# Activation table loaded first, one diagonal score group computed in full, last weights loaded at other points of the schedule

## The chip, the cores and the metric

The kernel runs on one core of a Trainium2 chip. The metric is the device time of one execution in microseconds (us). The engines are called by their profile names: PE is TensorE, DVE is VectorE, ACT is ScalarE, POOL is GpSimd (it issues most of the loads from memory here), SP is SyncE (it issues the transposing transfers here). An instruction issued to a queue for a transfer carries a q, as in SPq.

Kernels are compared by a ratio: the mean time of one kernel's fast runs over the mean of the other's fast runs of the same rounds. So a gain quoted from a ratio is not quite the difference of the medians. Gains in us are (1 - ratio) x 1260.

## The reference, cut to what matters

```python
# attention part: 8 batches, S = 3008 rows, D = 256, z has 64 columns
scores = (1.0 / S) * np.matmul(z, z.transpose(0, 2, 1))   # symmetric
attn = np.maximum(scores, 0.0) ** 2
x = (u * np.matmul(attn, v)).reshape(B * S, D)
# feed-forward part, d_ff = 2048
h = x @ moe_w_in
g = h * np.cos(h)
out = g @ moe_w_out
```

## The kernel before

Each batch is cut into 6 columns of 512 rows (c) and 6 row blocks of 512 (R); the last of each has 448. A group (b, c, R) is a 512x512 piece of the symmetric attention matrix: four matmuls, Relu, square, into a tile `a`. Off the diagonal, only the groups with R > c are computed as a rule, and the mirrored piece comes from a transposing transfer (`tt<-a`, a 512x512 tile). In the first three columns of batch 0 (`direct`) all groups are computed.

A diagonal group (R == c) is symmetric in itself. The kernel computes its upper part and mirrors the rest with three small transposing transfers inside the tile (`a<-a`), except in the `direct` columns:

```python
def direct(b, c, R):
    return b == 0 and c <= 2

def s_matmuls(b, c, R, p):
    ...
    diagonal = R == c and not direct(b, c, R)
    for k in ((0, 1), (3, 2) if diagonal else (2, 3))[p]:
        s0 = k if diagonal else 0          # diagonal: 512, 384, 256, 128 columns
        ...

def s_squares(b, c, R, p, banks):
    ...                                    # a tile from a ring of 9
    diagonal = R == c and not direct(b, c, R)
    if diagonal:
        for i in range(2):
            k = 2 * p + i
            nc.scalar.activation(rt[:, i, k * P:], banks[k][:, k * P:], AF.Relu)   # L240
            nc.vector.tensor_tensor(...)                                           # L241, the squares
            if k < K - 1:
                nc.sync.dma_start_transpose(                                       # L245, a<-a
                    t[:, k + 1:, k, :],
                    t[:, k, k + 1:, :].rearrange("p s w -> p (s w)"))
        ...
        return
    for i in range(2):
        ...
            nc.scalar.activation(rt[:, i, :], banks[k], AF.Relu)                   # L256
    nc.vector.tensor_tensor(...)                                                   # L258, the squares
    if p == 1:
        ...
        if R > c and not direct(b, R, c):
            nc.sync.dma_start_transpose(tt..., t...)                               # L265, tt<-a
```

The cosine is the Sin function with a bias of pi/2 (L348), followed by a product on DVE (`g`, L351). The order of PE is fixed by the program; each step has a time t, in which a column takes 8 units. A load is released when PE has reached the step before it. PE lines to know: L223 scores, L310 attention products, L344 input matmuls (x times w_in), L361 output matmuls (g times w_out).

```python
            for q in range(4):
                at(4 + 2 * q, 0, lambda q=q: load_w_in(q))
                at(15 + 2 * q, 0, lambda q=q: load_w_out(q))
        else:
            at(t - 3.5 * U, 0, lambda b=b: load_z(b))      # U = 8
    ...
    def prepare():
        nc.scalar.activation(dummy, pihalf, AF.Relu)       # first instruction of ACT
```

## Time and profile before

| | kernel before |
|---|---|
| median of 3 runs | 1260.18 us |
| span in the profile | 1256.7 us |
| PE busy | 99% of the span |
| waits of PE, all in the first 84 us | 14.7 us |

From the page of the kernel before: the first line is busy time and share of the span; the other two cut the span into 40 slices, with the busy share and the granted clock of PE in tenths.

```profile
PE 1238.2 (99%) x7533; PEld 680.4 (54%) x7533; DVE 782.0 (62%) x1391; ACT 845.6 (67%) x1610; POOL 146.0 (12%) x201
...
PE   8879999999999999999999999999999999999998
...
PEclk9979999999999999999999999999999999999999
```

PE has no room except in the first three slices (31 us each), and the third slice has a clock of 7 tenths. The waits of PE in the kernel before (who waited, for whom, us in all, times, longest):

```profile
PE acc L310 <- DMA a<-a: 6.4, 3, 5.1
PE w L223 <- DVE g L351: 3.0, 6, 1.3
PE acc L310 <- DVE x L331: 1.3, 1, 1.3
...
PE w L344 <- DVE g L351: 0.8, 1, 0.8
```

The largest wait is for the small transposes of a diagonal group. Which one, the timelines show. First PE in order of time (start, us, engine, line, operation, count; in brackets the idle time before it and what ended it):

```profile
63.07 3.30 PE L344 MATMUL w<-x,w_in_70 128*128 128x512 f16 x8 [0.75 <-DVE g L351]
66.21 0.38 PE L310 MATMUL acc<-a,v_66 128*128 128x512 f16 x1
71.65 0.59 PE L310 MATMUL acc<-a,v_66 128*128 128x512 f16 x1 [5.06 <-DMA a<-a]
72.92 0.59 PE L310 MATMUL acc<-a,v_66 128*128 128x512 f16 x1 [0.68 <-DMA a<-a]
74.19 2.29 PE L310 MATMUL acc<-a,v_66 128*128 128x512 f16 x5 [0.68 <-DMA a<-a]
...
84.46 0.60 PE L361 MATMUL w<-w_out_71,g 128*128 128x256 f16 x4
```

The products of column 3 begin at 66.21 us and stop after one matmul. Then the queue of SP, for the same stretch:

```profile
40.92 28.22 SPq L265 DMA_TRANSPOSE tt<-a  x5
69.31 3.74 SPq L245 DMA_TRANSPOSE a<-a  x3
73.10 4.19 SPq L265 DMA_TRANSPOSE tt<-a  x2
```

The three `a<-a` transposes of column 3's diagonal group are issued from 69.31 us on, after five large `tt<-a` transposes that held the queue for 28.22 us. DVE had the squares ready long before:

```profile
53.53 1.02 DVE L241 TENSOR_TENSOR a<-rt 128x512 f16<-128x512 f16 x4
59.33 0.69 DVE L258 TENSOR_TENSOR a<-rt 128x1024 f16<-128x1024 f16 x1 [4.79 <-DMA tt<-a]
...
63.53 1.89 DVE L258 TENSOR_TENSOR a<-rt 128x1024 f16<-128x1024 f16 x3
```

The squares of the diagonal group (L241) ended at 54.55 us. Then DVE stood 4.79 us, because its next group needed an `a` tile that a `tt<-a` transfer was still reading. ACT, at the same time:

```profile
49.11 1.28 ACT L348 ACT_TABLE_LOAD   x1
50.41 0.69 ACT L348 ACTIVATE c_661<-w,pihalf 128x512 f16<-128x512 f32 x1
```

A table load of 1.28 us stands before the first cosine. The windows view gives, for each stretch, its length, then the busy us of PE, PEld, DVE, ACT and POOL (instructions in brackets), then the granted clock, DMA share and GB/s.

```profile
61.00:62.00 1.00, 0.55 (x4) 0.18 (x2) 1.00 (x3) 1.00 (x3) 0.00 (x0) 1.00 1.60 158
62.00:63.00 1.00, 0.32 (x2) 0.10 (x1) 1.00 (x3) 1.00 (x3) 0.00 (x0) 0.78 1.56 169
63.00:64.00 1.00, 0.93 (x3) 0.37 (x3) 1.00 (x3) 1.00 (x3) 0.00 (x0) 0.50 1.51 194
...
77.00:78.00 1.00, 1.00 (x4) 0.31 (x3) 0.00 (x0) 0.00 (x0) 0.00 (x0) 0.50 1.15 218
```

The clock was halved twice: from about 62.6 to 66 us and from about 69.4 to 79.6 us (the edges are worked out from the mean clock of the stretches that hold them). The first of these stretches is 3.41 us long, the second 10.23 us. In the PE timeline, eight matmuls of L344 take 3.30 us at 63.07 us, where eight at full clock take 1.89 us.

### The profile page before, as it was taken

How to read it: one execution, taken by the hardware profiler on the slowest of the kernel's cores; microseconds unless marked ns; L12 is line 12 of the kernel's file. 1: busy time of each engine (PE TensorE's matmuls, PEld its weight loads, DVE VectorE, ACT ScalarE, POOL GpSimd, SP SyncE). 2: the span in 40 equal slices, each digit the busy share in tenths (PEclk: the TensorE clock that was granted, in tenths of full speed). 3: DMA queues.
4: the chain of work that ended last, by engine and by line, in shares of the span. 5: the costliest groups of instructions: out<-in, count | busy, mean ns of one | idle time of the engine just before them, and what ended most of it. 6: DMA issues, size and time to landing. Idle time of an engine off the chain costs nothing.

```text
span 1256.7 us, 20414 instructions
## 1 busy us (share of the span) xinstructions
PE 1238.2 (99%) x7533; PEld 680.4 (54%) x7533; DVE 782.0 (62%) x1391; ACT 845.6 (67%) x1610; POOL 146.0 (12%) x201
## 2 busy tenths in 40 slices
PE   8879999999999999999999999999999999999998
PEld 3335555555555555555555555555555555555556
DVE  8646656666666666666656666666666666666555
ACT  6646766667766676667766666776767666677646
POOL 3300101101020010200101001010010101100000
PEclk9979999999999999999999999999999999999999
DMA  9977858778576795868958679676695856957311
GB/s 162 161 127 132 130 98 118 122 122 133 104 111 116 118 133 107 121 119 114 135 97 116 122 124 141 90 122 113 116 146 102 116 110 109 156 94 113 71 33 44
DMA packets 485076, 145.05 MB, mean 115 GB/s; under 512 B 433264, under 2 KB 484976, under 8 KB 484976
## 3 DMA queue, kind: packets, MB, share of 16 engines
q1 hardware_dynamic: 357312, 88.92, 42.7%
q0 software_dynamic: 100400, 29.77, 24.1%
q10 hardware_dynamic: 27264, 25.06, 6.3%
q8 instruction: 59, 0.97, 0.3%
q14 instruction: 41, 0.34, 0.1%
HBM read 60.29 MB, written 24.64 MB: 68 GB/s over the span
## 4 chain that ended last, share of the span: by engine, by line
PE 96%; DMA 2%; DVE 1%; ACT 0%; SPq 0%; issue 0%; DVEq 0%
PE acc L310 37%; PE w L361 26%; PE w L344 26%; PE w L223 6%; DMA tt<-a 1%; PE acc L285 1%; DMA ut<-ust_62 1%; DVE g L351 0%; DMA x<-in_z_dram 0%; SPq L245 0%; DMA a<-a 0%; ACT zT_63 L196 0%; DVE a L258 0%; DVE x L331 0%; ACT rt L256 0%
## 5 line engine op out<-in xcount | busy, mean ns | idle before, releaser
L344 PE MATMUL w<-x,w_in_70 128*128 128x512 f16 x1504 | 447.9, 381 | 0.8 <-DVE g L351 0.8
L361 PE MATMUL w<-w_out_71,g 128*128 128x256 f16 x3008 | 448.6, 273 | 0.0
L361 PEld LDWEIGHTS <-g 128*128 128x128 f16 x3008 | 294.2, 98 | 191.6 <-issue 1.4
L256 ACT ACTIVATE rt<-w 128x512 f16<-128x512 f32 x485 | 251.2, 614 | 119.7 <-PE w L223 119.7
L258 DVE TENSOR_TENSOR a<-rt 128x1024 f16<-128x1024 f16 x252 | 172.4, 691 | 182.5 <-ACT rt L256 177.3
L344 PEld LDWEIGHTS <-w_in_70 128*128 128x128 f16 x1504 | 147.6, 98 | 61.1 <-issue 7.3
L90 POOL DMA_DIRECT2D ust_62<-in_u_dram x64 | 44.8, 704 | 400.1 <-PE acc L310 389.1
L240 ACT ACTIVATE rt<-w 128x512 f16<-128x512 f32 (+3 forms) x180 | 64.3, 449 | 39.8 <-PE w L223 39.8
L310 PEld LDWEIGHTS <-v_66 128*128 128x128 f16 x552 | 52.1, 98 | 68.4 <-issue 21.6
L310 PE MATMUL acc<-a,v_66 128*128 128x512 f16 x312 | 81.3, 385 | 7.7 <-DMA a<-a 6.4
L331 DVE TENSOR_TENSOR x<-acc,ut 128x64 f16<-128x64 f32 (+7 forms) x178 | 69.7, 432 | 27.7 <-PE acc L310 26.6
L310 PE MATMUL acc<-a,v_65 128*128 128x512 f16 x336 | 85.8, 380 | 0.0
L310 PEld LDWEIGHTS <-v_67 128*128 128x128 f16 x552 | 52.1, 98 | 59.3 <-issue 12.3
L310 PEld LDWEIGHTS <-v_65 128*128 128x128 f16 x552 | 51.6, 98 | 59.8 <-issue 12.2
L310 PEld LDWEIGHTS <-v_68 128*128 128x128 f16 x552 | 51.9, 98 | 57.7 <-issue 10.9
L310 PE MATMUL acc<-a,v_67 128*128 128x512 f16 x312 | 80.0, 383 | 0.0
L310 PE MATMUL acc<-a,v_68 128*128 128x512 f16 x312 | 79.2, 379 | 0.0
L368 ACT ACTIVATE ob<-w 128x256 f32<-128x256 f32 x188 | 73.0, 388 | 5.3 <-PE w L361 5.3
L241 DVE TENSOR_TENSOR a<-rt 128x512 f16<-128x512 f16 (+3 forms) x180 | 48.4, 322 | 44.1 <-ACT rt L240 44.1
L90 POOL DMA_DIRECT2D ust_61<-in_u_dram x48 | 36.5, 765 | 227.3 <-PE acc L310 219.8
L310 PE MATMUL acc<-tt,v_68 128*128 128x512 f16 (+1 forms) x240 | 62.2, 371 | 0.0
L310 PE MATMUL acc<-tt,v_67 128*128 128x512 f16 (+1 forms) x240 | 62.1, 371 | 0.0
(1547 smaller groups left out, 1400.1 us busy)
## 6 DMA issues: line engine op xcount, KB each, us to landing
out_dram<-ob ACTq DMA_DIRECT2D x92, 256.0 KB, 2.3
ust_61<-in_u_dram POOLq DMA_DIRECT2D x48, 128.0 KB, 4.0
ust_62<-in_u_dram POOLq DMA_DIRECT2D x32, 128.0 KB, 4.4
a<-a SPq DMA_TRANSPOSE x135, 2.9
v_65<-in_v_dram POOLq DMA_DIRECT2D x4, 512.0 KB, 6.0
v_66<-in_v_dram POOLq DMA_DIRECT2D x4, 512.0 KB, 6.5
v_68<-in_v_dram POOLq DMA_DIRECT2D x4, 512.0 KB, 6.4
v_67<-in_v_dram POOLq DMA_DIRECT2D x4, 512.0 KB, 6.1
```

Of the source, the lines that this page charges most:

```text
L90: hold(nc.gpsimd.dma_start(dst, src))
L223: chain(nc.tensor.matmul(sp[:, s0 * P:], zt[h, R * K + k + 1 - lo, :], zt[h, j0 + s0:j0 + K, :].rearrange("p j w -> p (j w)"), start=True, ...
L240: nc.scalar.activation(rt[:, i, k * P:], banks[k][:, k * P:], AF.Relu)
L241: nc.vector.tensor_tensor(t[:, k, k:, :].rearrange("p s w -> p (s w)"), rt[:, i, k * P:], rt[:, i, k * P:], ALU.mult)
L256: nc.scalar.activation(rt[:, i, :], banks[k], AF.Relu)
L258: nc.vector.tensor_tensor(t.rearrange("p s k w -> p k s w")[:, 2 * p:2 * p + 2], rv, rv, ALU.mult)
L285: chain(nc.tensor.matmul(accs[(b, c)][nh], vs(b, NG - 1)[h, G - 1, nh * P:(nh + 1) * P], a[h], start=False, stop=False))
L310: chain(nc.tensor.matmul(acc[nh][:, 0:wn], vs(b, j // G)[:, j % G, nh * P:(nh + 1) * P], a, start=(n == 0), stop=(n == NJ - 2)))
L331: nc.vector.tensor_tensor(x[:, nh, :], acc[nh][:, o:o + n], ut[:, nh, o:o + n], ALU.mult)
L344: chain(nc.tensor.matmul(hp, w_in16[:, k, ft * P:(ft + 1) * P], x[:, k, :], start=(k == 0), stop=(k == NDH - 1)))
L361: chain(nc.tensor.matmul(ys[m][:, 0:D], gs[(m, f4)][:, ft % FG, ts * P:(ts + 1) * P], w_out16[:, ft, :], start=(ft == 0), stop=(ft == NFT ...
L368: nc.scalar.activation(obs[m][:, i, :], ys[m][:, 0:D], AF.Copy, bias=0.0, scale=inv_s2)
```

## The change

Its intent: (A) load the table that holds the cosine at the start, where ACT has nothing to do; (B) compute column 3's diagonal group of batch 0 in full, so that it needs no transpose; (C) load the last weights, w_out, later, out of the way of the transposes. The whole diff:

```diff
@@ s_matmuls and s_squares
-        diagonal = R == c and not direct(b, c, R)
+        diagonal = R == c and (b, c) > (0, NC // 2)
@@ the schedule
-                at(15 + 2 * q, 0, lambda q=q: load_w_out(q))
+                at(17 + 2.5 * q, 0, lambda q=q: load_w_out(q))
@@ prepare
-        nc.scalar.activation(dummy, pihalf, AF.Relu)
+        nc.scalar.activation(dummy, pihalf, AF.Sin)
```

NC // 2 is 3, so the first line changes group (0, 3, 3) alone.

## The prediction

> **What bounds the kernel now.** TensorE: the page gives PE 99% of a 1256.7 us span, and the chain that ended last is 96% PE. After 84 us the view of waits shows no wait of PE at all. All that can be won lies before. There its waits sum to 14.7 us: 6.4 us for the transposes of a diagonal group ("DMA a<-a"), 3.8 us for VectorE's g, the rest mostly start-up.
>
> To this comes the clock. The windows view shows a granted clock of 0.50 from 62.3 to 66 us and from 70 to 79.5 us; 512-wide matmuls then stand 0.42 us apart instead of 0.22. The Trainium skill, "TensorE: Matmul & The Clock Gate" (Part 1), says the array halves its clock after about 3.4 us of idleness and needs as long a busy stretch to get it back; this trace agrees (half soon after the gap from 66.6 to 71.6 us, full 5 us after steady work resumes at 74.2). Estimate of what it costs: 3.6/2 + 5.3/2 = 4.4 us.
>
> **The parts of the change.**
>
> 1. Diagonal group of column 3 in full. Its three transposes wait in the SyncE queue behind five large tt transposes (40.9 to 69.1 us, 4 to 7.6 us each): squares ready at 54.5 us, transposes issued at 69.3 to 71.9 us. Without them PE goes on at 66 us. Removed: 6.4 us of wait and the second cold stretch, 2.6 us. Added: 768 matmul columns (under 0.3 us), and about a microsecond of ScalarE and VectorE.
>
> 2. The cosine table first. ScalarE's timeline shows two table loads of 1.28 us, at 1.27 us (nobody waits) and at 49.1 us, before the first cosine; none later, though Relu, Copy and Sin mix, so one should do. The Trainium skill, "ScalarE: Activation LUTs" (What ACT_TABLE_LOAD costs), gives 1283 ns; the trace agrees. PE waits 0.51 + 0.38 + 0.33 us behind it. Gain: 1.2 us.
>
> 3. w_out later. Four 256 KB loads are issued at 41.7 to 52.0 us, 10.7 us to landing, while the transposes crawl. VectorE stands 4.8 us (54.5 to 59.3) until a tt transpose frees its a buffer; this costs PE 2.5 us and the first half-clock stretch, 1.8 us. About two loads move behind that transpose; I expect it 2 to 3 us sooner. But part 2 brings PE there 1.2 us sooner, so I count half: 2 us of 4.3. The last load will be issued near 62 us and wanted near 73 us: just enough at 10.7 us, perhaps a wait of up to 2 us.
>
> **Sum.** 6.4 + 2.6 + 1.2 + 2 - 0.3 (columns) - 0.3 (late weights) = 11.6 us, all critical, since PE runs without a gap afterwards. Predicted 1260.2 - 11.6 = 1248.6 us; range 1245.5 to 1253.0. Chances: faster by over 2%: 0.01; within 2%: 0.985; slower: 0.005.
>
> **What would show it.** Right: no "DMA a<-a" among PE's waits; one table load, at the start; PEclk's slice of 7 back at 9; first output matmul near 73 us instead of 84.5; PE's work after it unchanged. Step 3 is wrong if VectorE still stands 4 us or more for tt and half clock near 60 us remains.
>
> **What would make it wrong.** PE, arriving sooner, waits for another transfer (w_out, u or tt not landed); the Relus need a second table load; contention so tight that tt lands no sooner and swallows part 2 (then the gain is about 8 us).

## The result and the profile after

| | before | after |
|---|---|---|
| median (6 runs each) | 1260.01 us | 1246.45 us |
| lowest to highest | 1257.53 to 1262.06 | 1244.05 to 1247.43 |
| ratio of the fast runs | | 0.9892, 95% interval 0.9878 to 0.9905 |
| span in the profile | 1256.7 us | 1244.6 us |

The gain is 13.6 us, 1.08%. The page of the changed kernel, the same lines:

```profile
PE 1234.4 (99%) x7533; PEld 680.0 (55%) x7533; DVE 782.0 (63%) x1389; ACT 844.7 (68%) x1609; POOL 145.8 (12%) x201
...
PEclk9999999999999999999999999999999999999999
```

PE's work has become 3.8 us shorter although matmul columns were added: both half-clock stretches are gone in this profile. That is one execution. The record also gives the mean granted clock of every timed run, from which the time at half clock can be estimated as 2 x (1 - clock) x span. The six runs of the changed kernel have 1.000 (twice), 0.999, 0.998 and 0.997 (twice), so four of them had about 2.5 to 7.5 us of half clock somewhere. The 34 runs of the kernel before in the rounds told of below have 0.993 to 0.997, that is about 17.6 to 7.5 us; the 12 at 0.993 took 1260.7 us on average, the 8 at 0.996 or 0.997 took 1258.0. So there is much less half clock than before, but not always none.

PE's waits in the changed kernel:

```profile
PE acc L310 <- DVE x L331: 2.6, 1, 2.6
...
PE w L344 <- DVE g L351: 0.8, 1, 0.8
PE w L223 <- DVE g L351: 0.4, 2, 0.2
```

There is no `DMA a<-a` any more, and the wait of the scores for g went from 3.0 to 0.4 us. The timelines of PE, SP, DVE and ACT of the changed kernel, in this order:

```profile
62.62 1.89 PE L344 MATMUL w<-x,w_in_70 128*128 128x512 f16 x8 [0.75 <-DVE g L351]
64.34 1.89 PE L310 MATMUL acc<-a,v_66 128*128 128x512 f16 x8
66.07 1.03 PE L310 MATMUL acc<-a,v_67 128*128 128x512 f16 x4
...
72.65 0.60 PE L361 MATMUL w<-w_out_71,g 128*128 128x256 f16 x4
```

```profile
43.29 35.32 SPq L265 DMA_TRANSPOSE tt<-a  x7
```

```profile
56.13 0.69 DVE L258 TENSOR_TENSOR a<-rt 128x1024 f16<-128x1024 f16 x1 [0.28 <-ACT rt L256]
58.88 0.69 DVE L258 TENSOR_TENSOR a<-rt 128x1024 f16<-128x1024 f16 x1 [2.06 <-ACT c_739 L348]
```

```profile
1.27 1.28 ACT L465 ACT_TABLE_LOAD   x1 [1.27 <-PEq L497]
```

The products of column 3 now run through, at full clock, and the first output matmul stands at 72.65 us instead of 84.46. SP issues seven large transposes in a row, with no small ones between them. DVE stands 2.06 us instead of 4.79. The profile puts that wait down to a cosine on ACT, but this DVE instruction needs no cosine. It is the group whose tile a `tt<-a` transfer must free: that transfer was issued at 47.39 us and took 11.4 us to land, which is 58.8 us, the moment DVE goes on; this is argued from the times, the view itself names the cosine. Before, the same transfer was issued at 44.74 us and took 14.5 us. So with the w_out loads moved (issued at 45.2 to 64.4 us instead of 41.7 to 52.0) it landed 3.1 us faster. All profiles told of bear this out: the same transfer took 13.4 to 14.5 us in all seven in which the w_out loads are where they were, and 8.7 to 11.8 us in the four in which only they, of the loads, were moved. The only table load is the one at 1.27 us.

Two points of time divide the profile: the first input matmul (47.85 us before, 50.23 after) and the first output matmul (84.46 and 72.65). The stretch between them shrank from 36.61 to 22.42 us, that is by 14.2 us. After it, both kernels need the same: 1172.2 and 1172.0 us. Before it, the changed kernel lost 2.4 us, by chance as far as can be told: the loss was complete when the transpose of u for column 2 was issued (39.59 and 41.97 us), ahead of the first w_out load of the kernel before (41.73 us), and up to there the two programs differ in the first table alone. One part is likely the clock at the start. The first eight 128x128 matmuls took 0.62 us in the one profile and 1.03 us in the other, and the first product began at 10.64 or 11.70 us. (The two do not always go together: `ab` has 1.03 us and 10.63, `queue2` 0.62 us and 11.01.) The Trainium skill, "TensorE: Matmul & The Clock Gate" (Part 1), says that the window that releases the clock is free-running and its moment varies from run to run. The runs here agree: in each of the 14 profiles told of, the recorded edges of half clock lie whole multiples of 3.41 us apart, on a grid that starts elsewhere in each; and six begin the products at 10.6 to 10.7 us and eight at 11.0 to 11.9, with no relation to the part of the change that they hold. (The clock's record says full speed there in both; the half clock is read from the length of the matmuls.) The rest is PE's wait before column 2 for the product with the transposed u, which was between nothing and 4.5 us. So one profile cannot rank kernels that differ by less than about 3 us; the stretch between the two points is the better measure, and the timed runs decide.

### The profile page after: what moved, and what is told of

The parts are those of the page before. It is cut to its first block, busy times and chain, and to the rows that moved or that the text cites. A ratio compares the mean times of both kernels' runs of the same rounds, so it can differ in the third digit from the quotient of the medians.

```text
span 1244.6 us, 20404 instructions
## 1 busy us (share of the span) xinstructions
PE 1234.4 (99%) x7533; PEld 680.0 (55%) x7533; DVE 782.0 (63%) x1389; ACT 844.7 (68%) x1609; POOL 145.8 (12%) x201
## 4 chain that ended last, share of the span: by engine, by line
PE 97%; DMA 2%; DVE 0%; ACT 0%; issue 0%; DVEq 0%; ACTq 0%
PE acc L310 37%; PE w L361 26%; PE w L344 26%; PE w L223 6%; DMA tt<-a 1%; DMA ut<-ust_62 1%; PE acc L285 1%; DMA x<-in_z_dram 0%; DVE g L351 0%; PE w L191 0%; DVE x L331 0%; ACT zT_63 L196 0%; ACT rt L256 0%; DVE a L258 0%; DVE zst L186 0%
## 5 line engine op out<-in xcount | busy, mean ns | idle before, releaser
L310 PEld LDWEIGHTS <-v_65 128*128 128x128 f16 x552 | 51.6, 98 | 60.0 <-issue 13.1
L310 PEld LDWEIGHTS <-v_67 128*128 128x128 f16 x552 | 51.9, 98 | 58.7 <-issue 11.1
```

The lines of the kernel that those rows point to most:

```text
L310: chain(nc.tensor.matmul(acc[nh][:, 0:wn], vs(b, j // G)[:, j % G, nh * P:(nh + 1) * P], a, start=(n == 0), stop=(n == NJ - 2)))
```

## The experiments

Two theories were set against each other. The theory of the gate: in the kernel before, column 3 waits for `a<-a` transposes that stand behind large ones in SP's queue; their time is set by the transfers, so whatever makes PE arrive sooner is worth nothing until the gate is gone. The rival: the stalls simply add up, each part bringing its own gain. A second rival: it is mainly the contention of the transfers, so loading w_out later would do most of it.

All outputs are right. Gains are against the kernel before of the same rounds, with 5 rounds asked for. The last column is the stretch from the first input matmul to the first output matmul in the one profile of each.

| run | what it holds | ratio (95% interval) | gain us | stretch us |
|---|---|---|---|---|
| (before) | | | | 36.61 |
| a_table | A | 1.0007 (0.9995 to 1.0019) | -0.9 | 35.18 |
| b_diag | B | 0.9912 (0.9899 to 0.9925) | 11.1 | 24.77 |
| c_wout | C | 0.9986 (0.9975 to 0.9998) | 1.8 | 33.50 |
| ab | A, B | 0.9896 (0.9878 to 0.9915) | 13.1 | 26.89 |
| ac | A, C | 0.9962 (0.9947 to 0.9978) | 4.8 | 34.52 |
| bc | B, C | 0.9896 (0.9882 to 0.9910) | 13.1 | 22.52 |
| (after) | A, B, C | 0.9892 (0.9878 to 0.9905) | 13.6 | 22.42 |
| queue | order of transposes, not achieved | 1.0010 (0.9998 to 1.0022) | -1.3 | 35.23 |
| queue2 | order of transposes | 0.9917 (0.9899 to 0.9936) | 10.5 | 24.77 |
| fill | needless matmuls in the gap | 0.9979 (0.9965 to 0.9992) | 2.6 | 34.86 |
| ut_early | after, u turned sooner | 0.9900 (0.9886 to 0.9915) | 12.6 | 22.40 |
| ut_z | after, u sooner and z later | 0.9885 (0.9871 to 0.9900) | 14.5 | 21.47 |
| z_late | after, z later | 0.9898 (0.9880 to 0.9915) | 12.9 | 21.47 |

### The parts alone and in pairs

Each takes the lines of the diff that belong to its parts, and nothing else. For A alone:

```diff
-        nc.scalar.activation(dummy, pihalf, AF.Relu)
+        nc.scalar.activation(dummy, pihalf, AF.Sin)
```

> The kernel before with the cosine table at the start, nothing else. Theory of the queue (the transposes of column 3's diagonal group stand behind five large transposes in the SyncE queue, and those are limited by the transfers): the 1.2 us that PE gains near 51 us is lost again at the next wait for a transpose, so 0 to 0.5 us faster in all; one table load, at the start; the wait of PE for a<-a grows by about as much as it arrives sooner. Rival (the stalls simply add up): 1.2 us faster.

Measured: no gain (1259.33 against 1259.96 us), and the table load at 49 us was gone. The waits of PE for g fell, but the gate stood nearly where it was: in its profile the `a<-a` transposes were issued at 69.90 us, 28.0 us after the products of column 2 began; before it was at 69.31, 28.8 us after. The wait at the gate did not grow as the theory expected (6.1 us against 6.4): in this profile the clock was halved from 61.75 to 78.82 us without a break, so PE came late. Its stretch is that of `queue` below (35.18 and 35.23 us), which has the schedule of the kernel before. So the times show that A alone brings next to nothing; that the gate ate it is argued. The interval does not exclude a gain of half a microsecond; it does exclude the 1.2 us of the rival.

> The kernel before with column 3's diagonal group in full, nothing else. Theory: 6.4 us of wait and the second half-clock stretch (2.6 us) go, 0.3 us of matmul columns are added: 8 to 9.5 us faster; the first half-clock stretch near 62 us and VectorE's wait of 4 to 5 us for tt stay. Rival (most of the gain comes from the weights loaded later, which eases the transfers): under 5 us.

Measured: 11.1 us, more than the theory's 8 to 9.5. The tt wait of DVE stayed, somewhat shorter than expected (3.35 us). The half-clock stretch near 62 us, which was to stay, did not appear in this profile, and the clocks of its four timed runs (1.000 or 0.999) leave room for one stretch of 3.4 us at most.

> The kernel before with the w_out loads later, nothing else. Theory: the tt transposes and so the a<-a transposes land 2 to 3 us sooner, the half-clock stretch after them stays: 2 to 3.5 us faster, PE still waits 4 us or more for a<-a. Rival (contention is the main cause): 7 us or more, with the wait for a<-a nearly gone.

Measured: 1.8 us, a little under the expected 2 to 3.5. The gate is still there, 26.0 us after column 2 began instead of 28.8; the waits in its profile say why so little came through.

```profile
PE acc L310 <- DMA a<-a: 7.8, 2, 7.2
...
PE w L223 <- DVE g L351: 1.2, 3, 0.5
```

The wait for g fell from 3.0 to 1.2 us, as the tt transfer frees DVE's tile sooner. PE then arrived at column 3 earlier (21.7 us after the start of column 2 instead of 25.7), and waited 7.8 us for the transposes instead of 6.4. The rival of contention (7 us or more) falls.

> Table first and diagonal group in full, w_out loaded as before. Theory: the table's 1.2 us are mostly swallowed by VectorE's wait for the tt transpose, which lands no sooner: 8.5 to 10 us faster than before, half clock near 60 us stays. Rival (stalls add up): the diagonal group alone plus 1.2 us.

Measured: 13.1 us, with an interval of 10.7 to 15.4 us. The theory's 8.5 to 10 us is a miss, as it was for B alone. Whether A adds nothing to B's measured 11.1 us or the rival's 1.2, the interval cannot tell. The half clock near 60 us was there, as expected:

```profile
60.00:61.00 1.00, 0.78 (x2) 0.14 (x2) 1.00 (x2) 1.00 (x2) 0.00 (x0) 0.72 1.60 158
61.00:62.00 1.00, 0.77 (x3) 0.20 (x2) 1.00 (x3) 1.00 (x3) 0.00 (x0) 0.50 1.59 159
...
66.00:67.00 1.00, 1.00 (x4) 0.31 (x3) 0.84 (x2) 0.63 (x1) 0.00 (x0) 0.50 1.46 171
```

> Table first and w_out later, diagonal group as before. Theory: nothing over w_out later alone (2 to 3.5 us faster than before), since the a<-a transposes gate PE and their time is set by the transfers. Rival (stalls add up): 1.2 us more than w_out later alone.

Measured: 4.8 us, 3.0 us more than C alone in other rounds; the theory expected no difference. The two intervals (2.8 to 6.7 and 0.3 to 3.2 us) just overlap, so this is a miss of the theory in the times, or scatter. The profile sides with the theory: the wait for the gate is the longest of all, and the stretch is no shorter than with C alone (34.52 against 33.50 us).

```profile
PE acc L310 <- DMA a<-a: 9.4, 3, 8.1
```

> Diagonal group in full and w_out later, table loaded before the first cosine as in the kernel before. Theory: 11.5 to 13 us faster than before; no half-clock stretch after 50 us; compared with the whole change it lacks 0.5 to 1.2 us. Rival (w_out later brings nothing once the group is in full): as the group alone, 8 to 9.5 us.

Measured: 13.1 us, just past the expected 11.5 to 13, and 0.5 us less than the whole change. No half-clock stretch after 50 us. The rival (C brings nothing once B is in) is not excluded by the times alone, 11.1 against 13.1 us in different rounds; the stretch went from 24.77 to 22.52 us.

The parts alone sum to -0.9 + 11.1 + 1.8 = 12.0 us, the whole brings 13.6. B is what counts.

### The place in the queue

Does the gate come from the transposes themselves, or from the place where they stand? The kernel before was to issue the three `tt<-a` of column 2 after the three `a<-a` of column 3's diagonal group, with the same transfers and arithmetic. In the first attempt the calls were only moved in the text of the program:

```diff
+                if (b, c) == (0, 2):
+                    later.append(turn)     # issued where (0, 3, 3) is done
+                else:
+                    turn()
```

> The kernel before with the three tt transposes of column 2 issued after the three transposes of column 3's diagonal group instead of before them; the same transfers, the same arithmetic. Theory (place in the SyncE queue): the a<-a transposes are issued near 59 us, land before PE arrives at 66 us, and 7 to 9 us are gained, as with the group in full. Rival (the transposes of the group cost by their traffic or by their own latency): under 2 us gained.

It gained nothing, but it was no test: SP's queue had the old order, since the order in which instructions are put on an engine is not the order of the text.

```profile
42.36 27.65 SPq L268 DMA_TRANSPOSE tt<-a  x5
70.18 3.74 SPq L246 DMA_TRANSPOSE a<-a  x3
```

The run serves as a repeat of the kernel before: the same schedule, with a wait of 7.8 us at the gate. The second attempt forces the order with a dependency on the last `a<-a` transpose (`lastd`); the lines that keep it are left out:

```diff
+                while later:
+                    after(later.pop(0)().ins, lastd[0], NOSYNC)
```

> The run 'queue' did not do what it was meant to: its SyncE queue had the old order (the five large tt transposes still ahead), since the issue order is not the order of the program's text. Here the order is forced: the three transposes of column 3's diagonal group stand behind two large tt transposes instead of five; same transfers, same arithmetic as before. Theory (place in the queue): they are issued before 60 us, PE at 66 us does not wait for them, 8 to 11 us are gained, as with the group in full (11.1 us measured). Rival (the group's transposes cost by traffic or by their own latency): under 3 us gained.

Measured: 10.5 us, without computing anything in full. SP's queue:

```profile
41.51 11.23 SPq L270 DMA_TRANSPOSE tt<-a  x2
54.77 3.82 SPq L247 DMA_TRANSPOSE a<-a  x3
58.64 15.99 SPq L270 DMA_TRANSPOSE tt<-a  x5
```

The small transposes were issued at 54.77 us, as soon as the squares were ready, with two large ones ahead of them and five behind. PE's waits hold no `a<-a` any more. So it was the place in the queue, not the transposes: moving them and removing them bring the same (10.5 and 11.1 us, intervals 8.1 to 12.7 and 9.5 to 12.7).

### The clock in the gap

The kernel before, with needless matmuls in the gap; their result is not read.

```diff
+        for i in range(22):
+            chain(nc.tensor.matmul(wp, w_in16[:, 0, 0:P], w_in16[:, 0, 0:CW], start=True, stop=True))
+    at(24.9, 2, filler)          # column 3's products begin at 25.0
```

> The kernel before with 22 needless 128x512 matmuls (results unread) put on PE just before column 3's products, so in the gap in which PE waits for the a<-a transposes. If the halved clock after that gap really costs 2.6 us, PE stays at full clock through the gap: 2 to 3.5 us faster although 4.7 us of work are added. Rival (the half clock hides under other waits): same or slower.

Measured: 2.6 us faster although 4.75 us of work were added. The size is the expected one, but the profile shows the mechanism only in part:

```profile
70.00:72.00 2.00, 0.38 (x1) 0.10 (x1) 0.00 (x0) 0.00 (x0) 0.00 (x0) 1.00 0.51 106
72.00:74.00 2.00, 0.63 (x2) 0.20 (x2) 0.00 (x0) 0.00 (x0) 0.00 (x0) 0.90 0.12 22
74.00:76.00 2.00, 2.00 (x6) 0.73 (x5) 0.00 (x0) 0.00 (x0) 0.00 (x0) 0.50 1.15 215
76.00:78.00 2.00, 2.00 (x9) 0.75 (x7) 0.00 (x0) 0.09 (x1) 0.00 (x0) 0.75 1.15 210
```

The clock stayed full through the gap, but then three waits (1.9, 0.9 and 0.9 us) remained and it was halved all the same from about 73.6 to 77 us, when PE had its data at last. So the run shows that work added into the gap costs nothing, and that half clock then starts later and lasts shorter (3.3 us past the last wait for `a<-a` instead of 5.4). The clocks of its five timed runs agree: 0.997 to 1.000, where the kernel before of the same rounds had 0.993 to 0.996. That the 2.6 us are the clock's is thus likely, not shown: this profile also had no half clock near 62 us, where the run changes nothing.

### Looking for a better version

What is left of PE's waits in the changed kernel is chiefly the one for the transposed u at the start of column 2 (2.6 us). `ut_early` turns u of column 1 sooner; `z_late` loads z of the next batch later, after the crowded stretch; `ut_z` does both.

```diff
-  at(t + c * U + (1 if b or c not in (1, 2) else -3 * c), 0, ...turn_u)
+  at(t + c * U + (1 if b or c not in (1, 2) else (-6.5, -6)[c - 1]), 0, ...turn_u)      # ut_early, ut_z
-  at(t - 3.5 * U, 0, ...load_z)      at(t - 2.5 * U, 0, ...turn_z)
+  at(t - (3.5 if b > 1 else 2.8) * U, 0, ...load_z)                                     # ut_z, z_late
+  at(t - (2.5 if b > 1 else 2.2) * U, 0, ...turn_z)                                     # ut_z, z_late
```

> The changed kernel, with the transpose of u for column 1 put into the SyncE queue before the first large tt transposes instead of after three of them. PE's wait at the start of column 2 for the product with u (1.3 us in the profile of before, 2.6 us in that of after) should go: 1.3 to 2.6 us faster than the changed kernel. It is lost again if the tt transposes, now later by one, hold VectorE up more at 57 us.

Measured: 12.6 us, no better than the changed kernel. DVE no longer waited for the transposed u, but all large transposes came later by one, and DVE waited for one of them at the same place:

```profile
41.74 1.29 DVE L258 TENSOR_TENSOR a<-rt 128x1024 f16<-128x1024 f16 x2 [4.55 <-DMA tt<-a]
42.95 1.28 DVE L331 TENSOR_TENSOR x<-acc,ut 128x512 f16<-128x512 f32 x2
```

> As the run before it, and z of batch 1 loaded some 18 us later (and turned some 8 us later), out of the stretch in which the tt transposes crawl. If the transfers still limit there, the waits of PE near 61 us (1.0 us) go: up to 1 us faster than the run before it. If z then arrives late for the scores of batch 1, slower.

> The changed kernel with z of batch 1 loaded some 18 us later and turned some 8 us later, and nothing else (u for column 1 is turned where it was). From 'ut_z' and 'ut_early': the stretch from the first input matmul to the first output matmul was 21.5 us with z late and 22.4 us without. Expected 0.5 to 1.5 us faster than the changed kernel, so 14 to 15 us faster than before; if the z load had not been in the way of the tt transposes, the same as the changed kernel (13.6 us).

Measured: 14.5 and 12.9 us; `ut_z` is 1.9 us faster than `ut_early` of the same rounds, more than the 1 us expected. In both profiles the stretch is 21.47 us, 0.95 us shorter than in the changed kernel, and in `z_late` the tt transfer that took 11.4 us takes 7.7, so z late does ease it a little. But the 14 to 15 us expected of `z_late` were missed: in time neither can be told from the changed kernel (13.6 us): the intervals overlap widely. No version was shown to be better.

## Why the prediction was right or wrong, point by point

The time was right: 1248.6 us predicted, 1246.45 measured, in the range of 1245.5 to 1253.0, near its fast end. "Within 2%" came true.

1. **Part 1, the gate (B): mechanism right, size too small.** "Its three transposes wait in the SyncE queue behind five large tt transposes" is shown by `queue2`. The terms 6.4 + 2.6 - 0.3 = 8.7 us measured 11.1 us alone. The step that failed is taking the wait and the first half-clock stretch as separate gains of separate parts. The gate opens when the transfers allow; whatever slows PE before it, costs nothing and only shortens the wait. In the profile of before, PE came late to the gate, partly because of the half clock from 62.6 us on (the prediction read 62.3), and waited 6.4 us. In `queue`, the same schedule without that half clock, it waited 7.8 us. The stretch there is 10.5 us longer than in `b_diag`, which agrees with the timed 11.1. The prediction's rule for the clock, half after about 3.4 us of idleness, fits the kernel before only roughly: the second half clock began at 69.4 us, 2.8 us into the gap, and the first, at 62.6 us, came with no gap over 1.33 us ahead of it.
2. **Part 2, the table (A).** "Gain: 1.2 us" was not found alone (-0.9 us, interval -2.4 to 0.6). The text's own warning, that the gain may be swallowed, came true; it named the tt wait, the theory here the gate, and no run shows which of the two it was. With B in place it brings 2.0 us more in the times (ab against b_diag) and 0.5 us (after against bc); neither is clear of scatter. The waits of PE just behind that table load were 0.96 us in b_diag and 0.36 us in ab, so about 0.6 us is what the profiles show.
3. **Part 3, w_out later (C).** "I expect it 2 to 3 us sooner": the tt transfer took 3.1 us less from issue to landing. The part brought 1.8 us alone and, over B, 2.0 us; counted were 2 us of 4.3 and -0.3. The clear fault is in the 4.3: half clock near 60 us does not follow from the tt wait each time. It came in the profiles of before, a_table and ab, and not in b_diag, queue or fill, which have nearly the same waits; in queue2 it came earlier, at 55.3 to 58.7 us. The test named for this step (VectorE standing 4 us or more, half clock remaining) came out in favour: 2.06 us, no half clock. As half clock comes and goes by itself, its absence in one profile proves little.
4. **The late last load.** No wait for w_out was seen; the 0.3 us set aside for it were not needed. It was issued at 64.37 us and took 8.8 us to land, at 73.2 us, half a microsecond after the first output matmul (72.65 us), which did not wait.
5. **What would show it.** No `a<-a` wait, one table load at the start, PEclk's slice back at 9, the first output matmul near 73 us (72.65), equal work afterwards: all five came out.

The sum of 11.6 us was 2 us short. Part 1's term makes up most of that (8.7 against 11.1).

What stays open: how 13.6 us divide between A and C, whose effects of 0.5 to 2 us are as large as the intervals; why A and C together gained 4.8 us in the times; and how much of the gap's cost is the clock.

## What to carry to other kernels

A small transfer that PE needs soon can be held up by large ones that nobody needs yet, if all stand in one queue: look at when its data was ready, when it was issued and what held the queue between, and then move it ahead or do without it. Stalls before such a gate must not be added to the gain of opening it: PE coming sooner waited longer (6.4 us before, 7.8 with C, 9.4 with A and C), and C alone brought 1.8 us where 2 to 3.5 were expected. One profile does not tell how often the clock is halved: look at the clock of every timed run. And when order in a queue is the point, look at the queue's order in the trace before believing the result: the order of the program's text was not it.

## What the Trainium skill lacked or had wrong

- "ScalarE: Activation LUTs" (What ACT_TABLE_LOAD costs): the load of 1283 ns is right (1.28 us here), but the drain of about 1380 ns that it adds to every switch was not seen. In the kernel before, the ACTIVATE ahead of the load ended at 49.09 us and the one behind it began at 50.41 us, 1.32 us for the whole switch.
- "TensorE: Matmul & The Clock Gate" (Part 1 and HAM oscillation): it speaks of an idle window or gap of about 3.4 us. In the kernel before the clock was halved at about 62.6 us with no gap longer than 1.33 us; PE had been idle for 2.0 of the 3.2 us ahead of it, in pieces. In b_diag 2.05 us idle out of 3.2 us, in the same place, did not halve it. The grid of 3.41 us fits this pair: all edges of a profile lie on it, and in b_diag (whose only recorded half clock, at 1246.24 us just after its last instruction, places the grid) the idle time falls into two windows, with 0.85 and 1.20 us, while in the kernel before one window holds all 2.0 us. Idle time alone does not decide, though: over the 14 profiles every window with more than 2.05 us idle was followed by half clock, but of those between 1.2 and 2.05 us some were (1.22 us in queue2) and some were not (2.05 us in c_wout, ahead of column 2). The page tells of a kernel in which short, frequent idle times make the clock oscillate (A second HAM failure mode), and gives no threshold for a part-idle window.
- "DMA: Bandwidth & Descriptors" (Anatomy of one DMA): its fit of 2.0 us + bytes/436e3 gives an estimate of 2.6 us for a 256 KB load issued from GpSimd. Next to a row of transposing transfers these loads took 10.7 us (median) to land, and the large transposes up to 15.4 us, in the kernel before. The page has no figure for loads and transposes that share the engines.
